# Sums of small products kept in PSUM with ScalarE copies, the products in another order, and the attention's VectorE and ScalarE work at other places

## The chip, the cores and the metric

The kernel runs on one core of one Trainium2 chip. The metric is the device time of one execution in microseconds (us). A core has five engines that run side by side, each through its own list of instructions in order: TensorE (matmul; PE in the profile, PEld its weight loads), VectorE (DVE), ScalarE (ACT), GpSimd (POOL), and SyncE (SP), whose queue issues all DMAs here. Matmul results go to PSUM, eight banks that TensorE, VectorE and ScalarE reach; all else lies in SBUF.

## The reference, cut to what matters

```python
# x: 8 batches x 8 heads x 512 x 64, state: 8 x 8 x 32 x 64
scores = scale * x @ state.T;   a  = softmax(scores);   xread = a @ state
scores2 = scale * state @ x.T;  a2 = softmax(scores2);  sread = a2 @ x
y = concatenate([xread, sread], axis=2)        # per batch 512 + 32 tokens
y = y.transpose(0, 2, 1, 3).reshape(4352, 512) # tokens x 512
h = y @ w_in                                   # 512 x 2048
g = h * sigmoid(1.702 * h)
out = g @ w_out                                # 2048 x 512, float32
```

## The kernel before, in words

**Per batch.** The 512 tokens of a batch (a key: 0 to 7) go through attention, the up product and the down product. Weights of the x side of the attention (a) are not multiplied with state on their own: M = state times w_in is made (att_M, 64 by 32 matmuls, four in the array at a time), and h is a times M. Keys 0 and 1 are computed in a first stage while the weights are unpacked; from key 1's down product on there is one loop over batches, `for b in range(1, B)`. In it the up product of batch b (up_strassen), the down product of batch b (strassen_two) and the attention of batch b + 1 (hooks_next) are interleaved. The last stage ("sr") does the 256 state tokens.

**Up.** up_strassen makes the up product with Strassen's seven products (Winograd's form) instead of eight, four column groups u = 0 to 3, products of 128x256 (L1113), with gelu on ScalarE (L1119, L1159 to L1171) and sums on VectorE (L1122 within it; s12 and s3, L567 to L573, for the sums S1, S2 that the down product needs). In it ScalarE copies one product (L1138) into a bank on which another product then accumulates. `between[u]` holds functions called at the end of group u; they come from `A[b]["sums"]`. Its last product and sums (`rest`) are called inside P1, at hook P1.1.

**Down.** strassen_two makes seven products, P1, P2, P5, P6, P3, P7, P4 in this order, and from key 2 on each of them is itself seven small products (lowly, strassen_low; key 1 has P1 and P2 as whole products, L751). A small product is 4 matmuls of 128x128 in float32, which the profile shows as 8 (L691). In all there are 47 small Strassens. A small Strassen uses three banks x, y, z. The sums of left-hand blocks are VectorE instructions written in line L758 (`tt`): steps1 (P1), steps2 (P2), sums_of(S1), sums_of(S2) and third_of (P5, P6), s4 (the block a12 minus S2), steps12 (P3), steps3 (P7), steps4 (P4). The results of the small products are put together on VectorE (`add`, L696) and ScalarE (L702, L706), with p and u2, two 128x128 pieces of the tile pu, as room for a partial sum.

**Order.** It is written out by hand: every engine works in program order. `at(i)` after the i-th small product calls the functions that belong to the product itself (`own`, `first`) and then the hooks of the name "P2.3", say (P2, after its third small product); "P1", "run" (after P3), "T" (after steps3) are hooks between products. hooks_next(b) fills the names with the attention of the next batch: att_state, att_scores, load_x, att_M 0 and 1, att_blocks (transposes of the scores), then two softmaxes. That of the state side is att_s_max (VectorE), att_s_exp (ScalarE, with a table load, L372), att_s_norm; its result goes out to DRAM and back in another order (eT_out, four issues of 128 KB; eT_in; eT_turn). That of the x side is x_max, x_sub, x_exp (ScalarE, L425), x_sum, x_inverse, x_scale, and x_back, which gives aT. Then the sums of aT and M for the next up stage follow (up_sums: steps 1 to 4 the T-sums of aT; 6 and 9 S1, 7 and 10 S2, 8 and 11 a difference in M's place, 13 and 14 S4).

**Loads.** The next batch's x comes in squares (load_x_squares, L150, 16 issues of 64 KB), issued after P4 into a tile that P4 still read, and VectorE turns them in place (turn_x, L156, four transposes of 128x512). The sums of w_out's blocks for each of the seven products are made once, in key 1's time, and kept in DRAM (`outside`, low_made, low_away); low_load brings three pieces of 256 KB back into one of two rooms (low_a, low_b) each time.

The order of the small products before: q1, q5, q2, q6, q7, q3, q4 in P1 and P2 (`late`), q1, q6, q2, q5, q7, q3, q4 in the others.

Of the kernel before, what the change touches and what calls it, by code (L numbers as in the profile page):

```python
# [10 lines left out]
FP32 = mybir.dt.float32  # L11
# [3 lines left out]
ALU = mybir.AluOpType  # L15
# [5 lines left out]
def kernel(  # L21
# [89 lines left out]

    pu = konst.tile([P, 2, P], FP32, name="pu")
    zeros = free[-1][:, 0].bitcast(mybir.dt.bfloat16)[:, :FC]
# [37 lines left out]

    def turn_x(b):

        A[b]["xT"] = xsq[b]
        for j in range(NPR):
            nc.vector.transpose(xsq[b][:, j], xsq[b][:, j])  # L156
# [487 lines left out]
    def low_load(k, i):  # L644

        for n in (1, 0, 2):
            nc.sync.dma_start(low[:, 3 * i + n], outside[k][:, FC * n : FC * (n + 1)])
# [33 lines left out]

    def strassen_low(left, right, bank, R, at, late=False):

        b11, t3, b21, b22, t1, t2, t4 = right
        a11, a12, a21, a22, s1, s2, s4 = left
        p, u2 = (pu[:, i] for i in range(2))
        x, y, z = (v[:, :P] for v in bank)

        def product(ps, lhs, rhs, first):
            for f in range(QF):  # L690
                nc.tensor.matmul(  # L691
                    ps, lhs[f], rhs[:, f], start=(first and f == 0), stop=(f == QF - 1), skip_group_check=True
                )

        def add(out, x0, x1):
            nc.vector.tensor_tensor(out=out, in0=x0, in1=x1, op=ALU.add)  # L696

        c11, c12, c21, c22 = (R[:, i, P * k : P * (k + 1)] for i in range(2) for k in range(2))

        def q1():  # L700
            product(x, a11, b11, True)
            nc.scalar.copy(p, x)  # L702

        def q2():
            product(x, a12, b21, False)
            nc.scalar.copy(c11, x)  # L706

        def q6():
            product(y, s2, t2, True)
            add(u2, y, p)  # L710

        def q5():
            product(z, s1, t1, True)
            add(c22, z, p)

        def q7():
            product(y, a21, t3, False)
            add(c22, y, c22)

        def q3():  # L720
            product(z, s4, b22, False)
            add(c12, z, u2)

        def q4():
            product(y, a22, t4, False)
            add(c21, y, p)

        for i, q in enumerate((q1, q5, q2, q6, q7, q3, q4) if late else (q1, q6, q2, q5, q7, q3, q4)):
            q()
            at(i + 1)  # L730

    def strassen_two(key, dst, hooks, a4):
# [48 lines left out]

        def sums_of(*pairs):
            for s, (r1, r2, r4) in pairs:
                tt(r1, whole(s, 1, 0), whole(s, 1, 1))
            for s, (r1, r2, r4) in pairs:
                tt(r2, r1, whole(s, 0, 0), ALU.subtract)
            for s, (r1, r2, r4) in pairs:
                tt(r4, whole(s, 0, 1), r2, ALU.subtract)

# [32 lines left out]

        def lowly(name, left, right, kept, banks, R, own, late=False):
            def at(i):
                for fn in own.get(i, ()):
                    fn()
                hook(f"{name}.{i}")

            b11, t3, b21, b22 = halves_of(right)
            strassen_low(left, (b11, t3, b21, b22, *kept), banks, R, at, late)  # L830

# [4 lines left out]
        if key == 1:  # L836
            product(bank(0), A_of(0, 0), B11, "P1")
            nc.scalar.copy(k1, bank(0))
        else:

            m = [mpool.tile([P, NG, FC], FP32, tag=f"M{i}", name="spare_M") for i in range(2)]
            left1, left2 = (v[:, i] for v in m for i in range(2)), None
            w1, w2, w4, p1 = left1
            steps1, left1 = sums(y_of(0, 0), [four(v) for v in (w1, w2, w4)])
            p1 = p1.rearrange("p (r n) -> p r n", r=2)
            for fn in steps1:
                fn()
            o, h0, h1 = low_banks()
            lowly("P1", left1, B11, low_b, [h0, o, h1], p1, {}, True)
            nc.scalar.copy(k1, p1)  # L850
            low_load(5, 1)
            t = apool.tile([P, NG, S], FP32, tag="aT", name="left2_0")
            v = apool.tile([P, NG, SCH, P], FP32, tag="eT", name="left2_1").rearrange("p g c q -> p g (c q)")
            *w, w3 = (four(x[:, i]) for x in (t, v) for i in range(2))
            steps2, left2 = sums(y_of(NU, 0), w, w3)
            for fn in steps2:
                fn()
            hook("P1")
        *r, p5 = spare_M()
        r = [four(v) for v in r]  # L860
        p5 = p5.rearrange("p (r n) -> p r n", r=2)
        if key == 1:
            sums_of((S1, r), (S2, (q1, q2, q4)))
            third_of(S1)
            product(bank(1), A_of(0, 1), B21, "P2")
            tt(osb, bank(1), k1)
        else:
            o, h0, h1 = low_banks()
            own2 = {2: [lambda: sums_of((S1, r))], 4: [lambda: third_of(S1)], 5: [lambda: sums_of((S2, (q1, q2, q4)))]}
            lowly("P2", left2, B21, low_a, [h0, o, h1], osb, own2, True)  # L870
            low_load(2, 0)
            tt(osb, osb, k1)
# [6 lines left out]
        hook("P2")  # L879
        first = [lambda: s4(0), lambda: s4(1), lambda: third_of(S2), lambda: s4(2), lambda: s4(3)]  # L880
        o, h0, h1 = low_banks()

        def at(i):
            for fn in first[i - 1 : i]:
                fn()
            hook(f"P5.{i}")
# [58 lines left out]
    def hooks_next(b):  # L945
# [18 lines left out]
        else:  # L964
            at(p2, att_M1, b)
        at(p2, att_blocks, b)
        at(p2, att_s_max, b)
        at(p2, att_s_exp, b)
        at(p2, eT_out, b)
        at("P2a" if first else "P2", x_max, b, 0)  # L970
        at("P2a" if first else "P2", x_sub, b, 0)
        at("P5.1", x_exp, b, 0)
        at("P5.6", att_s_norm, b)
        at("P5.6", x_max, b, 1)
        at("P5.7", x_sub, b, 1)
        at("P6.1", x_exp, b, 1)
        steps = up_sums(b)

        A[b]["sums"] = {0: steps[9:11], 1: [steps[11], steps[14]]}
        attention = [  # L980
            ("P6.1", x_sum, 0), ("P6.3", x_sum, 1), ("P6.3", x_inverse), ("P6.4", x_scale, 0),
        ]
        attention += [
            ("P6.6", x_scale, 1), ("P3.3", x_back, 0), ("P3.4", x_back, 1), ("P3.5", eT_turn, 0), ("P3.6", eT_turn, 1),
            ("P5", eT_in), ("run", att_sread), ("run", att_M, 3, True), ("run", att_M, 2),
        ]
        names = {"T": range(5), "P7.5": (5, 6), "P7.6": (7,), "P4.1": (8,), "P4.5": (12, 13)}
        for name, fn, *args in attention:
# [351 lines left out]
    for b in range(1, B):  # L1340
# [6 lines left out]
        if b + 1 < B:  # L1347
            if b > 1:
                turn_x(b + 1)
            hooks = hooks_next(b + 1)  # L1350
# [56 lines left out]
```

## Time and profile before

| | |
|---|---|
| time of three runs | 756.40, 758.07, 757.12 us; median 757.12 |
| the profiled execution | 758.99 us, span 757.2 us, mean granted TensorE clock 0.988 |
| busy | PE 705.7, DVE 603.7, ACT 263.6, POOL 0.8 us |
| small products L691 | in groups by tile, 128x128, about 278 ns each, pipelined |
| copies of the small products | L702 264 ns x33 and x14 in another tile, L706 |
| adds of the small products | L696, about 280 ns |
| DMA | 87.39 MB, mean 115 GB/s, 42.0% of 16 engines |

How to read it: the span is the time from the first instruction to the last of one profiled execution. In a timeline row stand start, duration, engine, line, operation, the tile written and those read, the shapes, the count of merged instructions, and in brackets how long the engine stood idle before and what ended it. PE's durations are modelled and overlap: eight matmuls of 128x128 that follow one another start 0.11 us apart. In a row of a window stand its length, busy time and instructions of PE, PEld, DVE, ACT and POOL, then the granted TensorE clock, the share of the DMA engines and GB/s. "issue" as a releaser is time for which the profile shows no other cause.

### The profile page before, as it was taken

To read this page: it belongs to the slowest core of one execution; us is meant where nothing else is said; L and a number is where in the kernel's file an instruction comes from. 1 tells how busy PE (TensorE), PEld (TensorE's weight loads), DVE (VectorE), ACT (ScalarE), POOL (GpSimd) and SP (SyncE) were. 2 spreads that over 40 slices of the span, in tenths; PEclk is the share of its full clock that TensorE was granted. 3 is DMA by queue.
4 is the path that set the end of the run, shared out by engine and by line. 5 is a ranking of instruction groups with operands and counts; after the bars stand their busy time and mean duration, and the time that the engine had idled before them with its cause. 6 is when DMAs were issued, how large, how long until landed. Compare 5 with 4: busy or idle time off the path is not lost.

```text
span 757.2 us, 13522 instructions
## 1 busy us (share of the span) xinstructions
PE 705.7 (93%) x5261; PEld 569.3 (75%) x5263; DVE 603.7 (80%) x1328; ACT 263.6 (35%) x536; POOL 0.8 (0%) x8
## 2 busy tenths in 40 slices
PE   8899999999898899889997999889997999899997
PEld 3333544479786799779985998769986998789995
DVE  6997999999957896869768995789677985688540
ACT  4796410131264224531274125432363126200320
POOL 0000000000000000000000000000000000000000
PEclk9999999999999999999999999999999999899999
DMA  9830344267441764075434744085416540132000
GB/s 231 331 113 28 113 152 103 110 187 176 154 74 54 177 176 106 12 162 156 143 57 98 182 140 101 29 181 168 119 25 133 173 141 16 34 119 82 32 1 29
DMA packets 148527, 87.39 MB, mean 115 GB/s; under 512 B 114416, under 2 KB 128240, under 8 KB 148464
## 3 DMA queue, kind: packets, MB, share of 16 engines
q1 hardware_dynamic: 148464, 86.53, 42.0%
q8 instruction: 42, 0.69, 0.4%
q14 instruction: 21, 0.17, 0.1%
HBM read 68.94 MB, written 17.56 MB: 114 GB/s over the span
## 4 chain that ended last, share of the span: by engine, by line
PE 69%; DVE 17%; ACT 6%; DMA 3%; issue 3%; SPq 0%; DVEq 0%; ACTq 0%
PE low L691 16%; PE o L691 11%; PE o L1113 11%; PE o L544 7%; PE h L526 7%; PE upx L1113 5%; DVE g L758 3%; PE M L320 3%; DVE spare_M L758 3%; PE o L587 2%; PE upw L1113 2%; DVE xsq L156 2%; ACT M L462 1%; ACT e L372 1%; DMA out_dram<-osb 1%
## 5 line engine op out<-in xcount | busy, mean ns | idle before, releaser
L691 PE MATMUL low<-w_out,g 128*128 128x128 f32 x416 | 56.2, 278 | 12.2 <-ACT pu L702 11.2
L691 PEld LDWEIGHTS low<-w_out,g 128*128 128x128 f32 x416 | 51.3, 192 | 17.8 <-ACT pu L702 12.2
L1113 PE MATMUL o<-ta,M 128*128 128x256 f32 x192 | 49.9, 382 | 0.0
L1113 PE MATMUL upx<-aT,M 128*128 128x256 f32 x192 | 49.3, 379 | 0.0
L691 PE MATMUL low<-low,g 128*128 128x128 f32 x336 | 44.4, 275 | 0.0
L702 ACT COPY pu<-low 128x128 f32<-128x128 f32 x33 | 8.7, 264 | 97.7 <-PE low L691 65.2
L691 PEld LDWEIGHTS low<-low,g 128*128 128x128 f32 x336 | 40.9, 192 | 0.0
L1113 PEld LDWEIGHTS o<-ta,M 128*128 128x128 f32 x192 | 35.5, 190 | 6.0 <-ACT g L1159 1.6
L1113 PEld LDWEIGHTS upx<-aT,M 128*128 128x128 f32 x192 | 36.0, 190 | 4.6
L691 PE MATMUL low<-sums,later 128*128 128x128 f32 x280 | 37.9, 279 | 0.9 <-DVE pu L696 0.9
L691 PEld LDWEIGHTS low<-sums,later 128*128 128x128 f32 x280 | 34.6, 194 | 1.9 <-DVE pu L696 1.8
L462 ACT COPY M<-M 128x512 f32<-128x512 f32 x59 | 30.7, 595 | 14.4 <-PE M L320 14.4
L1119 ACT ACTIVATE g<-o 128x512 f32<-128x512 f32 (+1 forms) x56 | 31.3, 559 | 10.7 <-PE o L1113 10.7
L691 PE MATMUL o<-w_out,g 128*128 128x128 f32 x160 | 23.3, 290 | 11.5 <-DVE pu L696 11.5
L691 PEld LDWEIGHTS o<-w_out,g 128*128 128x128 f32 x160 | 20.2, 198 | 17.7 <-DVE pu L696 12.6
L529 ACT ACTIVATE g<-h 128x512 f32<-128x512 f32 x24 | 14.0, 591 | 54.7 <-PE h L526 54.7
L320 PE MATMUL M<-w_in,stT 64*32 64x512 f32 x472 | 31.9, 594 | 0.0
L1122 DVE TENSOR_TENSOR o<-upw,g 128x512 f32<-128x512 f32 x18 | 12.6, 700 | 24.0 <-ACT g L1159 24.0
L526 PE MATMUL h<-low,M 128*128 128x512 f32 x64 | 29.5, 596 | 1.5 <-DVE low L408 1.5
L1113 PE MATMUL o<-ta,ms 128*128 128x256 f32 x120 | 30.8, 379 | 0.0
L526 PE MATMUL h<-aT,M 128*128 128x512 f32 x64 | 28.7, 599 | 1.4 <-ACT M L462 1.4
L691 PE MATMUL low<-low,spare_M 128*128 128x128 f32 x160 | 22.0, 280 | 7.7 <-issue 6.1
(248 smaller groups left out, 1620.1 us busy)
## 6 DMA issues: line engine op xcount, KB each, us to landing
low<-low SPq DMA_DIRECT2D x108, 256.0 KB
low<-low SPq DMA_DIRECT2D x11, 768.0 KB
later<-in_moe_w_out_dram SPq DMA_DIRECT2D x16, 512.0 KB
xn<-in_x_dram SPq DMA_DIRECT2D x28, 256.0 KB
w_out<-in_moe_w_in_dram SPq DMA_DIRECT2D x12, 512.0 KB
xsq<-in_x_dram SPq DMA_DIRECT2D x96, 64.0 KB
out_dram<-osb SPq DMA_DIRECT2D x18, 256.0 KB
out_dram<-later SPq DMA_DIRECT2D x14, 256.0 KB
```

Of the source, the lines that this page charges most:

```text
L156: nc.vector.transpose(xsq[b][:, j], xsq[b][:, j])
L320: nc.tensor.matmul(ps[g][st], A[b]["stT"][rows, st], rhs(rows, j), start=True, stop=True)
L462: nc.scalar.copy(m[:, g], ps[g])
L526: nc.tensor.matmul(hps, lhs[i], rhs[i], start=(i == 0), stop=(i == n - 1))
L529: nc.scalar.activation(out=G[key, f // 2][:, f % 2, :ntok], in_=hps, func=AF.Gelu_apprx_sigmoid)
L544: nc.tensor.matmul(ops, G[key, f // 2][:, f % 2, P * r : P * (r + 1)], w_out[:, f], start=(f == 0), stop=(f == NF - 1))
L587: nc.tensor.matmul(ps[:, r], lhs[f][:, P * r : P * (r + 1)], rhs[:, f], start=(first and r == 0 and f == 0), stop=(f == HF - 1), skip_grou ...
L691: nc.tensor.matmul(ps, lhs[f], rhs[:, f], start=(first and f == 0), stop=(f == QF - 1), skip_group_check=True)
L758: nc.vector.tensor_tensor(out=out, in0=x0, in1=x1, op=op)
L1113: nc.tensor.matmul(ps[:, k], lhs[i][:, o : o + P], rhs[i], start=(first and k == 0 and i == 0), stop=(i == n - 1), skip_group_check=True,)
L1119: nc.scalar.activation(out=dst, in_=src, func=AF.Gelu_apprx_sigmoid)
L1122: nc.vector.tensor_tensor(out=out, in0=ps, in1=x, op=ALU.add)
```

## The change

The three banks now hold the sums as well. ScalarE copies the first product from x into y, and q6 accumulates on it there; z holds q5 and then q3; y holds q1 + q6, then q7 is added, then q4. What was a VectorE add with p or u2 becomes a ScalarE copy of a bank (c22, c12, c21); two adds stay (c22 and c12). The order is q1, q5, q6, q2, q7, q3, q4 in all seven. The tile pu goes, and low_load takes its three pieces in the order 0, 1, 2.

Around it: turn_x of the next batch moves from before P1 into the up stage, two transposes at the end of group 1 and two at the end of group 2. P2's sums (steps2) move from between P1 and P2 into P1. The sums of S1 are spread over P2, and those of S2 move from P2 into P5. The state side's att_s_max goes from P1's end into P2.1, att_s_exp and eT_out to P2.3, att_s_norm from P5.6 to P6.1. The x side moves later as a whole, with x_scale at T and x_back at P7.5, and the up sums move behind it (P7.6 to P4.6).

```diff
-    pu = konst.tile([P, 2, P], FP32, name="pu")
...
-    def turn_x(b):
+    def turn_x(b, *js):
         A[b]["xT"] = xsq[b]
-        for j in range(NPR):
+        for j in js or range(NPR):
             nc.vector.transpose(xsq[b][:, j], xsq[b][:, j])
...
-        for n in (1, 0, 2):
+        for n in range(3):
             nc.sync.dma_start(low[:, 3 * i + n], outside[k][:, FC * n : FC * (n + 1)])
...
-    def strassen_low(left, right, bank, R, at, late=False):
+    def strassen_low(left, right, bank, R, at):
...
-        def q1():
-            product(x, a11, b11, True)
-            nc.scalar.copy(p, x)
-        def q2():
-            product(x, a12, b21, False)
-            nc.scalar.copy(c11, x)
-        def q6():
-            product(y, s2, t2, True)
-            add(u2, y, p)
-        def q5():
-            product(z, s1, t1, True)
-            add(c22, z, p)
-        def q7():
-            product(y, a21, t3, False)
-            add(c22, y, c22)
-        def q3():
-            product(z, s4, b22, False)
-            add(c12, z, u2)
-        def q4():
-            product(y, a22, t4, False)
-            add(c21, y, p)
-        for i, q in enumerate((q1, q5, q2, q6, q7, q3, q4) if late else (q1, q6, q2, q5, q7, q3, q4)):
-            q()
-            at(i + 1)
+        product(x, a11, b11, True)
+        nc.scalar.copy(y, x)
+        at(1)
+        product(z, s1, t1, True)
+        nc.scalar.copy(c22, z)
+        at(2)
+        product(y, s2, t2)
+        nc.scalar.copy(c12, y)
+        at(3)
+        product(x, a12, b21)
+        nc.scalar.copy(c11, x)
+        at(4)
+        product(y, a21, t3)
+        add(c22, y, c22)
+        at(5)
+        product(z, s4, b22)
+        add(c12, z, c12)
+        at(6)
+        product(y, a22, t4)
+        nc.scalar.copy(c21, y)
+        at(7)
...
-        def sums_of(*pairs):
...
+        def sums_of(s, rooms):
+            r1, r2, r4 = rooms
+            return [
+                lambda: tt(r1, whole(s, 1, 0), whole(s, 1, 1)),
+                lambda: tt(r2, r1, whole(s, 0, 0), ALU.subtract),
+                lambda: tt(r4, whole(s, 0, 1), r2, ALU.subtract),
+            ]
...
-            o, h0, h1 = low_banks()
-            lowly("P1", left1, B11, low_b, [h0, o, h1], p1, {}, True)
-            nc.scalar.copy(k1, p1)
-            low_load(5, 1)
...
             steps2, left2 = sums(y_of(NU, 0), w, w3)
-            for fn in steps2:
-                fn()
+            o, h0, h1 = low_banks()
+            own1 = {3: steps2[:1], 4: steps2[1:2], 6: steps2[2:3], 7: steps2[3:]}
+            lowly("P1", left1, B11, low_b, [h0, o, h1], p1, own1)
+            nc.scalar.copy(k1, p1)
+            low_load(5, 1)
             hook("P1")
...
+        sums1, sums2 = sums_of(S1, r), sums_of(S2, (q1, q2, q4))
         if key == 1:
-            sums_of((S1, r), (S2, (q1, q2, q4)))
+            for i in range(3):
+                sums1[i]()
+                sums2[i]()
...
-            own2 = {2: [lambda: sums_of((S1, r))], 4: [lambda: third_of(S1)], 5: [lambda: sums_of((S2, (q1, q2, q4)))]}
-            lowly("P2", left2, B21, low_a, [h0, o, h1], osb, own2, True)
+            own2 = {2: sums1[:1], 4: sums1[1:2], 5: sums1[2:], 6: [lambda: third_of(S1)]}
+            lowly("P2", left2, B21, low_a, [h0, o, h1], osb, own2)
...
-        first = [lambda: s4(0), lambda: s4(1), lambda: third_of(S2), lambda: s4(2), lambda: s4(3)]
+        first = {i + 1: [lambda u=u: s4(u)] for i, u in zip((0, 1, 4, 5), range(NU))}
+        first[3] = [lambda: third_of(S2)]
+        if key > 1:
+            first[1].insert(0, sums2[0])
+            first[2].append(sums2[1])
+            first[4] = sums2[2:]
...
         at(p2, att_blocks, b)
-        at(p2, att_s_max, b)
-        at(p2, att_s_exp, b)
-        at(p2, eT_out, b)
-        at("P2a" if first else "P2", x_max, b, 0)
-        at("P2a" if first else "P2", x_sub, b, 0)
-        at("P5.1", x_exp, b, 0)
-        at("P5.6", att_s_norm, b)
-        at("P5.6", x_max, b, 1)
-        at("P5.7", x_sub, b, 1)
-        at("P6.1", x_exp, b, 1)
+        at("P2a" if first else "P2.1", att_s_max, b)
+        p3 = "P2b" if first else "P2.3"
+        at(p3, att_s_exp, b)
+        at(p3, eT_out, b)
...
+        if b + 1 < B:
+            for i in range(NPR):
+                A[b]["sums"].setdefault(1 + i // 2, []).append((turn_x, (b + 1, i)))
         attention = [
-            ("P6.1", x_sum, 0), ("P6.3", x_sum, 1), ("P6.3", x_inverse), ("P6.4", x_scale, 0),
+            ("P6.1", att_s_norm), ("P6.1", x_max, 0), ("P6.2", x_sub, 0), ("P6.3", x_exp, 0), ("P6.6", x_max, 1),
+            ("P3.1", x_sub, 1), ("P3.3", x_exp, 1), ("P3.4", x_sum, 0), ("P3.5", eT_turn, 0), ("P3.6", eT_turn, 1),
+            ("P3.7", x_sum, 1), ("P3.7", x_inverse),
+            ("P5", eT_in), ("run", att_sread), ("run", att_M, 3, True), ("run", att_M, 2),
+            ("T", x_scale, 0), ("T", x_scale, 1), ("P7.5", x_back, 0), ("P7.5", x_back, 1),
         ]
-        attention += [
-            ("P6.6", x_scale, 1), ("P3.3", x_back, 0), ("P3.4", x_back, 1), ("P3.5", eT_turn, 0), ("P3.6", eT_turn, 1),
-            ("P5", eT_in), ("run", att_sread), ("run", att_M, 3, True), ("run", att_M, 2),
-        ]
-        names = {"T": range(5), "P7.5": (5, 6), "P7.6": (7,), "P4.1": (8,), "P4.5": (12, 13)}
+        names = {"P7.6": range(5), "P4.1": (5, 6), "P4.3": (7,), "P4.5": (8,), "P4.6": (12, 13)}
...
         if b + 1 < B:
-            if b > 1:
-                turn_x(b + 1)
             hooks = hooks_next(b + 1)
```

More of the change, by code (lines that the diff above doesn't have):

```diff
@@ L680, in low_third, with product @@
         T_of(b12, b22, b12)
-    def strassen_low(left, right, bank, R, at, late=False):
+    def strassen_low(left, right, bank, R, at):
         b11, t3, b21, b22, t1, t2, t4 = right
         a11, a12, a21, a22, s1, s2, s4 = left
-        p, u2 = (pu[:, i] for i in range(2))
         x, y, z = (v[:, :P] for v in bank)
-        def product(ps, lhs, rhs, first):
+        def product(ps, lhs, rhs, first=False):
             for f in range(QF):
@@ L821, in sums, with lowly @@
             ], (parts(0, 0), parts(1, 0), parts(0, 1), parts(1, 1), *(blocks(v) for v in rooms))
-        def lowly(name, left, right, kept, banks, R, own, late=False):
+        def lowly(name, left, right, kept, banks, R, own):
             def at(i):
@@ L829, in lowly @@
             b11, t3, b21, b22 = halves_of(right)
-            strassen_low(left, (b11, t3, b21, b22, *kept), banks, R, at, late)
+            strassen_low(left, (b11, t3, b21, b22, *kept), banks, R, at)
         def four(v):
@@ L879, in strassen_two @@
         hook("P2")
[L880 removed]
+        first = {i + 1: [lambda u=u: s4(u)] for i, u in zip((0, 1, 4, 5), range(NU))}
[4 more added lines that the diff above has]
+            first[4] = sums2[2:]
         o, h0, h1 = low_banks()
         def at(i):
[L884 removed]
+            for fn in first.get(i, ()):
                 fn()
```

6 lines of the change are left out of this document (removed).

## The prediction

> **What bounds the kernel now.** I read the page first, then the waits, the chain, and one batch on the timeline of each engine.
>
> ```profile
> span 757.2 us, 13522 instructions
> PE 705.7 (93%) x5261; PEld 569.3 (75%) x5263; DVE 603.7 (80%) x1328; ACT 263.6 (35%) x536; POOL 0.8 (0%) x8
> ```
>
> The page makes TensorE the bound, with at most 7% of the span to win beside any change of its work; this change alters no matmul. The waits (engine, line, releaser; total, times, longest) say who stops it:
>
> ```profile
> PEld o L691 <- DVE pu L696: 18.1, 12, 3.7
> PEld low L691 <- ACT pu L702: 12.2, 5, 2.4
> ```
>
> Both are the small products of L691, waiting for the tile pu. The chain gives the period of a batch, at the same step of five batches' up stage:
>
> ```profile
> 295.03 1.00 PE o L1113 x4
> 378.96 1.00 PE o L1113 x4
> 461.67 1.00 PE o L1113 x4
> 544.39 1.00 PE o L1113 x4
> 628.33 1.00 PE o L1113 x4
> ```
>
> Periods: 83.93 (key 3), 82.71, 82.72 and 83.94 us (key 6). I follow key 4, TensorE's timeline (start, duration; in brackets the wait):
>
> ```profile
> 397.93 1.05 PE L691 MATMUL low<-w_out,g 128*128 128x128 f32 x8
> 398.82 1.03 PE L1113 MATMUL o<-ta,M 128*128 128x256 f32 x4
> 401.38 1.13 PE L691 MATMUL low<-low,spare_M 128*128 128x128 f32 x8 [1.53 <-issue]
> 406.00 1.16 PE L691 MATMUL o<-w_out,g 128*128 128x128 f32 x8 [1.60 <-DVE pu L696]
> 408.88 1.09 PE L320 MATMUL o<-xsq,stT 64*32 64x512 f32 x16
> 411.62 1.16 PE L691 MATMUL low<-w_out,g 128*128 128x128 f32 x8
> 415.94 1.16 PE L691 MATMUL low<-w_out,g 128*128 128x128 f32 x8 [2.25 <-ACT pu L702]
> 421.30 1.06 PE L691 MATMUL low<-sums,later 128*128 128x128 f32 x8
> 428.85 1.06 PE L691 MATMUL low<-sums,later 128*128 128x128 f32 x8
> 444.47 1.16 PE L691 MATMUL o<-w_out,g 128*128 128x128 f32 x8
> 457.19 1.03 PE L1113 MATMUL upx<-aT,M 128*128 128x256 f32 x4
> ```
>
> P1 starts at 397.93, attention at 408.88, P2 at 411.62, P5 at 421.30, P6 at 428.85, P7 at 444.47, the next up stage at 457.19. From 444.47 on, 14 products and one transpose take 12.72 us: 0.9 us each with no stop to speak of. P1 and P2 need 14 x 0.9 = 12.6, the four L1113 matmuls 0.87, attention 2.74, a transpose 0.1: 16.3 us. They take 23.37, so 7.1 us are waiting. P5 takes 7.55 for 6.3 of work: 1.2 more. The rest runs dense. So about 8.3 of the 82.7 us are there to win, all in P1, P2 and P5.
>
> **The change, part by part.** VectorE in key 4:
>
> ```profile
> 390.17 0.70 DVE L1122 TENSOR_TENSOR o<-upw,g 128x512 f32<-128x512 f32 x1 [1.61 <-ACT g L1159]
> 395.35 0.70 DVE L1122 TENSOR_TENSOR o<-upw,g 128x512 f32<-128x512 f32 x1 [1.95 <-ACT g L1159]
> 398.49 2.48 DVE L156 STREAM_TRANSPOSE xsq<-xsq 128x512 f32<-128x512 f32 x4
> 400.89 0.72 DVE L758 TENSOR_TENSOR spare_M<-g,g 128x256 f32<-128x256 f32 x2
> 403.54 0.69 DVE L567 TENSOR_TENSOR later<-g,g 128x512 f32<-128x512 f32 x1
> ```
>
> *Transposes (turn_x).* Four at 0.62 stand ahead of P1's sums; they go two by two into holes of 1.61 and 1.95 us in the up stage: 1.24 fits each, cost nothing, if x has landed. Without that cover VectorE would stand there and hold the L1122 add behind it. The load:
>
> ```profile
> 377.58 8.38 SPq L150 DMA_DIRECT2D xsq<-in_x_dram  x16
> 387.50:388.00 0.50, 0.50 (x5) 0.42 (x4) 0.50 (x2) 0.50 (x2) 0.00 (x0) 1.00 0.00 0
> ```
>
> Issues end at 385.96, and from 387.5 the DMA share (next to last column) is 0.00. The first hole opens at 390.17 - 1.61 = 388.56: 1 us to spare. The load hangs on the end of the previous P4, as the up stage does, so it moves with it.
>
> *P1.* VectorE starts the eight L758 sums at 398.49 instead of 400.89 (2.65 for all), so the first pair is there at 399.2, before TensorE's slot at 398.82 + 0.87 = 399.69. The 1.5 goes. The 1.6 goes too: the product after the first one into y now waits for a ScalarE copy with another product between. Late next is VectorE: 398.49 + 2.65 + 1.95 (three of L567 to L573 at 0.65) + 1.33 (two of the four steps of P2's sums, now inside P1, half of 2.65) = 404.4 before it comes to the add into c22, done at 404.7; the last product's slot, after the ones ahead of it at 0.9, is 404.3. New wait 0.45 (behind it stands all of the attention's TensorE work); the attention starts at about 405.65, 3.2 earlier.
>
> *Seed and copies.* Of five VectorE adds per small Strassen two stay; three become copies, and pu goes: 47 x 3 = 141. The nearest rows:
>
> ```profile
> L702 ACT COPY pu<-low 128x128 f32<-128x128 f32 x33 | 8.7, 264 | 97.7 <-PE low L691 65.2
> L1138 ACT COPY o<-upx 128x512 f32<-128x512 f32 x24 | 13.8, 576 | 26.6 <-PE upx L1113 26.2
> ```
>
> ScalarE gains 141 x 0.264 = 37 us (35 to 40% of the span), beside matmuls. No row copies 128x128 from PSUM to PSUM: between 0.264 and the 0.576 of L1138's four times larger one; I take 0.27, since the form differs from L702 in the target alone and L1138's large copy is no dearer than a common one. Whether the round trip is hidden:
>
> ```profile
> 412.99 1.28 ACT L372 ACT_TABLE_LOAD   x1
> 414.28 0.69 ACT L372 ACTIVATE e<-o,mx 128x512 f32<-128x512 f32 x1
> 415.62 0.26 ACT L702 COPY pu<-low 128x128 f32<-128x128 f32 x1
> 417.13 0.27 ACT L706 COPY osb<-low 128x128 f32<-128x128 f32 x1 [1.25 <-PE low L691]
> ```
>
> The copy at 417.13 starts 0.03 after its product (415.94 + 1.16); the product at 415.94 starts 0.06 after the copy that ends at 415.88. So product, copy, next product is 1.06 + 0.03 + 0.27 + 0.06 = 1.42 us, and with one product between there are 1.79: margin 0.37 (0.06 at 0.576). In ScalarE's queue the waiting seed copy has only the next copies behind it, which need later products anyway, and at P1.1 the last gelu. The add into c22 before the last product has the same distance, as it has now.
>
> *P2.* Today the first copy stands behind four copies of M and the softmax's table load and exps (412.99 to 415.62). The change puts the exps behind the third product. The seed copy then follows the M copies directly, and the 2.25 goes. The exps run between the copies into c12 and c11: P2 starts at 405.65 + 2.74 = 408.4, its third product two slots later ends near 411.35; copy to 411.65; 2.63 of table and exps to 414.3, c11's copy to 414.6. P5's first product reuses that bank, slot about 414.8: just hidden. VectorE has the S1 sums one by one, none late.
>
> *P5.* Its 1.2 was VectorE's, with S2's sums and the attention ahead of the adds. What stands there after the change, five s4 and third steps and three sums at 0.61 and two adds at 0.2, is 5.3 us in 6.3, and no more than two of them between two adds: hidden, and P6 starts at 421.15 instead of 428.85.
>
> *P6 to P4, softmax moved later.* The x part's maxima go to P6, x_scale to T, x_back to P7.5, T-sums to P7.6. The exps of x wait for x_sub, which VectorE does one product earlier, so ScalarE's copies behind them are not held. From P3.6 VectorE has no hole: its second eT_turn ends near 433.9, x_sum and inverse 1.3, four steps3 2.65, two x_scale 1.2, four steps4 2.65, and the add for c22 is done near 442.0; TensorE's slot for P7's last product is 442.2. Two x_back 1.3, the add 0.2, four T-sums 1.5, then in P4 five sums of 0.6, and its add at 448.1 against a slot at 448.5. Hidden, by 0.2 and 0.4; without that cover each 0.1 is paid in full. M's third and S4 come after it, and the up stage needs them only at its fifth and seventh product, 4 us on.
>
> *DMA queue.* eT_out stays ahead of low_load(2, 0), which P6's second product now needs at about 422. eT_out issues when the exps end, 414.5 for some 3 us; 512 KB at the rate of the x load (1 MB from 377.6 to 387.5) is 5 us, so the first low tile lands near 421. Margin 1 us; today it is 7. The new order of its three pieces is the order of use.
>
> *The sum.* Key 4: 23.37 + 7.55 become 16.3 + 0.45 + 6.4 and 0.1 of restart: 7.7 us. Keys 2 to 6: 38.5. Keys 3 and 6 lose their extra 1.2 as well:
>
> ```profile
> 333.00:336.80 3.80, 3.42 (x18) 3.12 (x17) 2.18 (x4) 0.27 (x1) 0.00 (x0) 0.55 0.93 137
> 647.29 1.05 PE L691 MATMUL low<-w_out,g 128*128 128x128 f32 x8
> 655.41 2.07 PE L691 MATMUL o<-w_out,g 128*128 128x128 f32 x8 [3.52 <-DVE pu L696]
> 655.50:660.50 5.00, 5.00 (x24) 5.00 (x25) 0.58 (x2) 0.00 (x0) 0.00 (x0) 0.50 0.00 0
> 670.40 1.47 PE L691 MATMUL low<-sums,later 128*128 128x128 f32 x8
> ```
>
> In key 3's row the granted clock is 0.55 right after the waits of P1 and P2. With these gone, 2 x 1.2 = 2.4.
>
> Key 7 has no attention; P1 and P2 take 23.1 us (647.29 to 670.40) for 13.5 of work. The clock is 0.50 for 5 us behind a wait of 3.5, which costs 2.5. VectorE has four more sums at P1.2 there (2.4), so by key 4's count, 249.36 later, the add is done at 404.7 + 2.4 + 249.4 = 656.5, against a slot at 653.6: 2.9 of wait stay. P2's wait goes, and of the slow clock I keep half, 1.25, since the wait before it is a little shorter: 23.1 - 13.5 - 2.9 - 1.25 - 0.1 = 5.3.
>
> Key 1 has no small P1 and P2, and VectorE is its bound in P7 and P4:
>
> ```profile
> 189.15 0.68 DVE L1275 TENSOR_TENSOR low<-w_out 128x512 f32<-128x512 f32 x1
> 191.81 0.75 DVE L758 TENSOR_TENSOR later<-g,g 128x256 f32<-128x256 f32 x2
> ```
>
> low_made and low_third take 2.66 us (189.15 to 191.81) ahead of P7's sums and as much again inside P4. x_scale and x_back (2.5), and the later x_sum and inverse (1.3), join them; six adds (1.2) leave, and M's third and S4 (1.2) move behind P4. So VectorE comes to P4's last adds about 1.4 us later than today, and TensorE with it: -1.5.
>
> Sum: 38.5 + 2.4 + 5.3 - 1.5 = 44.7. The profiled execution had 758.99 (span 757.2), 0.25% above the median 757.12 of three. 758.99 - 44.7 = 714.3; against the median 712.4. I say 713.
>
> **Rivals.** *VectorE takes TensorE's place as bound.* For it: the margins 0.2 and 0.4 in P7 and P4 and the 0.45 in P1. If it comes 1 us late there and at P3, 2 to 3 us per batch return, 10 to 18 in all: 723 to 731.
>
> *A queue delays P5 or P6.* The exps hold c11's copy, or eT_out holds the low tiles beyond the 1 us: 1 to 2 us per batch for five, 718 to 723.
>
> *The round trip decides, slower than before.* If accumulating on a bank that ScalarE wrote costs much more than the 1.42, every small Strassen pays twice (seed, copy of y): 47 x 2 x the excess over 1.79. It eats the 44 us when the copy takes 0.37 + 0.47 longer, 1.1 us; at 1.3 the time is 757 - 44 + 62 = 775. L1138's 0.576 and the dense up stage that uses such a seed speak against it.
>
> *No change.* All of the 7.7 per batch would have to come back as waits of other engines; VectorE's case at 2.5 times its price would do it, and no row shows that much.
>
> *The clock stays whole in key 7.* If a wait of 2.9 us is too short to halve it, the 1.25 kept above goes: 711.5. For it: 2.9 is shorter than the 3.5 of today. Against it: key 3's 0.55 came after several shorter waits close together. The Trainium skill, "TensorE: Matmul & The Clock Gate", Part 1, has the clock halve after an idle window of about 3.4 us and come back after a busy one as long; by that rule this rival would hold, while key 3's row does not fit so sharp an edge.
>
> **How the numbers follow.** The forecast (709 to 717) has 0.45, the whole clock 0.15, VectorE as bound 0.2, a queue 0.11, slower 0.06, no change 0.03. A difference within 0.2% (1.5 us) can't be told from none here. With no new wait in keys 2 to 6 (0.55 x 5), none in key 1 and the whole clock the time would be about 706; the range goes from there to the end of VectorE's case, 705 to 731. Faster 0.91, same 0.03, slower 0.06.
>
> **What would show it.** The waits on pu are gone; L691 waits total under 10 us in keys 2 to 6. Periods near 75.0, equal for keys 3 to 5, granted clock 1.00 there. P1 keeps about 0.5 before its last product, released by VectorE. L156 stands in the up stage with no wait on DMA. ScalarE near 300 us busy, VectorE near 575. Wrong if L691 waits for ScalarE, for low tiles at P6, or if VectorE's add releases the last product late in P7 and P4.

## The result, and the profile after

The changed kernel takes 718.0 us (median; 717.4 to 718.5). Against 757.4 us of the kernel before on the same chip the ratio is 0.9481, interval 0.9464 to 0.9497: 5.2% faster. The forecast was 713, range 705 to 731. The profiled execution had 717.44 us, span 715.7, so 41.5 us of span went where the sum had 44.7.

The page after, busy times of the engines:

```profile
span 715.7 us, 13574 instructions
PE 692.5 (97%) x5263; PEld 562.2 (79%) x5263; DVE 570.0 (80%) x1187; ACT 298.8 (42%) x677; POOL 0.8 (0%) x8
```

ScalarE's 141 more instructions (536 to 677) and 35.2 us more are the copies, VectorE's 141 fewer the adds; the forecast had 37 and "near 300" and "near 575". TensorE's busy share rose from 93 to 97%, with the same matmuls. Its waits at the small products, now L689 (engine, line, releaser; total, times, longest), and the step of the chain that gave the period before:

```profile
PE o L689 <- DVE spare_M L694: 4.7, 6, 2.9
PE low L689 <- DMA low<-low: 2.4, 2, 2.2
PE low L689 <- DVE g L694: 2.4, 1, 2.4
PE low L689 <- DVE later L694: 1.6, 1, 1.6
```

```profile
214.14 0.99 PE o L1104 x4
252.98 4.53 DMA low<-low
289.54 1.00 PE o L1104 x4
364.89 1.00 PE o L1104 x4
439.87 1.00 PE o L1104 x4
514.85 1.00 PE o L1104 x4
553.72 6.53 DMA low<-low
592.27 1.00 PE o L1104 x4
```

The waits on pu (18.1 and 12.2) are gone. Of the first row 2.9 are key 7's and the other five 0.36 each, in keys 2 to 6; with the DMA's 2.4 these keys wait 4.2 us, where the forecast had under 10. The last two rows are key 1's. The periods are 75.40 (key 2), 75.35, 74.98, 74.98 and 77.42 us (key 6), where before they were 82.7 to 83.9. One thing is new: in keys 2 and 6 a DMA for the low tiles stands in the chain, where none stood in these keys before.

Key 4 on TensorE's timeline, from P1 (383.86) to the next up stage (435.39):

```profile
383.86 1.05 PE L689 MATMUL low<-w_out,g 128*128 128x128 f32 x8
385.61 1.05 PE L689 MATMUL low<-low,spare_M 128*128 128x128 f32 x8
388.40 1.06 PE L689 MATMUL o<-w_out,g 128*128 128x128 f32 x8
390.70 1.16 PE L689 MATMUL o<-low,g 128*128 128x128 f32 x8 [0.36 <-DVE spare_M L694]
394.53 1.16 PE L689 MATMUL low<-w_out,g 128*128 128x128 f32 x8
400.91 1.06 PE L689 MATMUL low<-sums,later 128*128 128x128 f32 x8
407.16 1.06 PE L689 MATMUL low<-sums,later 128*128 128x128 f32 x8
422.67 1.16 PE L689 MATMUL o<-w_out,g 128*128 128x128 f32 x8
435.39 1.03 PE L1104 MATMUL upx<-aT,M 128*128 128x256 f32 x4
```

The brackets of 1.53, 1.60 and 2.25 are gone, and one of 0.36 stands ahead of P1's last product. P1 to P5 takes 400.91 - 383.86 = 17.05 us, from 23.37; P5 takes 6.25, from 7.55; P6 to P7 15.51, from 15.62, and P7 to the up stage 12.72, as before.

Where the 41.5 us came from, with the same marker of the chain in every kernel (the step printed above, first at 214.14):

| us | before | sums alone | places alone | changed |
|---|---|---|---|---|
| start to key 1's marker | 212.3 | 211.8 | 217.0 | 214.1 |
| keys 2 to 6 | 416.0 | 400.1 | 392.6 | 378.1 |
| key 7 and the last stage | 128.9 | 120.4 | 126.9 | 123.4 |

The columns "sums alone" and "places alone" are the first two experiments.

### The profile page after: what moved, and what is told of

It reads as the page before. It is cut to its first block, busy times and chain, and to the rows that moved or that the text cites. A ratio compares the mean times of both kernels' runs of the same rounds, so it can differ in the third digit from the quotient of the medians.

```text
span 715.7 us, 13574 instructions
## 1 busy us (share of the span) xinstructions
PE 692.5 (97%) x5263; PEld 562.2 (79%) x5263; DVE 570.0 (80%) x1187; ACT 298.8 (42%) x677; POOL 0.8 (0%) x8
## 4 chain that ended last, share of the span: by engine, by line
PE 82%; DVE 11%; DMA 3%; ACT 2%; issue 1%; SPq 0%; DVEq 0%; ACTq 0%
PE low L689 22%; PE o L689 12%; PE o L1104 12%; PE o L543 8%; PE h L525 7%; PE upx L1104 5%; PE M L319 4%; PE o L586 2%; PE upw L1104 2%; PE o L738 2%; DMA low<-low 2%; DVE spare_M L745 1%; PE o L319 1%; DVE later L567 1%; PE warm L124 1%; DVE g L745 1%
## 5 line engine op out<-in xcount | busy, mean ns | idle before, releaser
L689 PE MATMUL low<-w_out,g 128*128 128x128 f32 x416 | 55.2, 279 | 0.0
L689 PEld LDWEIGHTS low<-w_out,g 128*128 128x128 f32 x416 | 51.4, 195 | 4.5 <-issue 4.2
L689 PE MATMUL low<-low,g 128*128 128x128 f32 x336 | 43.7, 276 | 6.3 <-DMA low<-low 2.4
L689 PEld LDWEIGHTS low<-low,g 128*128 128x128 f32 x336 | 40.3, 192 | 7.2 <-issue 2.9
L689 PE MATMUL low<-sums,later 128*128 128x128 f32 x280 | 35.8, 275 | 0.0
L689 PEld LDWEIGHTS low<-sums,later 128*128 128x128 f32 x280 | 33.6, 192 | 0.1
L543 PE MATMUL o<-w_out,g 128*128 128x512 f32 x64 | 28.5, 594 | 0.0
L543 PE MATMUL o<-w_out,sums 128*128 128x512 f32 x64 | 28.3, 592 | 0.0
L1150 ACT COPY g<-o 128x512 f32<-128x512 f32 (+1 forms) x28 | 15.6, 555 | 25.6 <-PE o L1104 25.4
L525 PEld LDWEIGHTS h<-aT,M 128*128 128x128 f32 x64 | 11.8, 190 | 18.3 <-issue 12.2
L689 PE MATMUL o<-low,g 128*128 128x128 f32 x152 | 21.3, 285 | 4.7 <-DVE spare_M L694 4.7
```

The source lines that it names most:

```text
L525: nc.tensor.matmul(hps, lhs[i], rhs[i], start=(i == 0), stop=(i == n - 1))
L543: nc.tensor.matmul(ops, G[key, f // 2][:, f % 2, P * r : P * (r + 1)], w_out[:, f], start=(f == 0), stop=(f == NF - 1))
L689: nc.tensor.matmul(ps, lhs[f], rhs[:, f], start=(first and f == 0), stop=(f == QF - 1), skip_group_check=True)
L1150: nc.scalar.copy(c12, Y(u))
```

## The experiments

**The new small Strassen alone** (psum_only: the sums in PSUM, the copies and the new order of products in the kernel before, attention and sums where they were).

```diff
 # kernel before, with the new body of strassen_low (three lines written as one)
-        for i, q in enumerate((q1, q5, q2, q6, q7, q3, q4) if late else ...):
+        product(x, a11, b11, True); nc.scalar.copy(y, x); at(1)
+        product(z, s1, t1, True); nc.scalar.copy(c22, z); at(2)
...
```

> The kernel before with the new small Strassen alone (sums in PSUM, new order, pieces loaded in the order of use); all attention and VectorE work stays where it was. My theory: the 1.5 us wait in P1 is the transposes ahead of its sums and P2's 2.3 us is the softmax's exps ahead of ScalarE's first copy, so both stay; only P1's second wait (1.6), most of P5's 1.2 and 0.5 in P2 go. Period of keys 2 to 6 about 79.5 instead of 82.7, time 735 to 741. Rival, the sums in PSUM carry the gain and the new places only tidy up: period 76 or less, time 720 to 726.

Measured: 734.23 us, ratio 0.9684 (0.965 to 0.9718), span 732.3: 0.8 us below the theory's range, far from the rival's. What TensorE still waits for in key 3:

```profile
313.61 1.13 PE L689 MATMUL low<-low,spare_M 128*128 128x128 f32 x8 [1.53 <-issue]
326.31 1.16 PE L689 MATMUL o<-low,left 128*128 128x128 f32 x8 [2.26 <-ACT o L698]
```

The 1.60 of P1 is gone: that product no longer needs VectorE's add into pu. The 1.53 ahead of P1's second product stays, and so does P2's wait, as 2.26. It is P2's third product in both kernels: before, it waited for the ScalarE copy into pu that empties its bank, now it waits for the copy into o on which it accumulates, and both copies stand behind the same softmax instructions. A PSUM sum doesn't help while the copy that makes it is queued behind the exps.

**The new places alone** (places_only: the changed kernel with the old small Strassen and pu).

```diff
-        product(x, a11, b11, True); nc.scalar.copy(y, x); at(1)
...
+        for i, q in enumerate((q1, q5, q2, q6, q7, q3, q4) if late else ...):
```

> The changed kernel with the old small Strassen (pu, five VectorE adds, two copies, the old orders of products and of low pieces), the work around it at its new places. My theory: the waits behind transposes and exps are gone without the PSUM sums as well; P1 keeps about 1.5 us for VectorE's adds behind the sums, and the three adds more per small Strassen (0.6 us) use up the margins of 0.2 and 0.4 us in P7 and P4. Period about 77.5, time 725 to 733. Rival, the places bring nothing without the ScalarE copies: 745 or more.

Measured: 738.15 us, 0.9728 (0.9687 to 0.9768), span 736.4: slower than the range. Its TensorE rows in keys 3 and 7:

```profile
320.82 1.16 PE L691 MATMUL o<-w_out,g 128*128 128x128 f32 x8 [1.67 <-DVE pu L696]
637.29 2.08 PE L691 MATMUL o<-w_out,g 128*128 128x128 f32 x8 [4.19 <-DVE pu L696]
```

In keys 2 to 6 it gave 23.4 us; of P1's and P2's waits those for VectorE's adds are left, 1.67 in P1 and 0.38 in P2. What was missed lies at the ends: VectorE keeps five adds per small Strassen, and key 1's marker comes 4.7 us later, of which 1.7 are a stretch of half clock (granted clock 0.50 from 209.42 to 212.83); key 7 has a 4.19 us wait. The two halves of the change are 15.9 and 23.4 us in keys 2 to 6, 39.3 together, and the whole gave 37.9: in the steady keys they add up almost fully, as each removes other waits. In key 1 the sums take load off VectorE and the places put it on: -0.5 and +4.7 alone (+3.0 without the half clock), +1.8 together. In key 7 and the last stage the sums alone give 8.5 us, more than the whole change's 5.5: the wait ahead of P1's last product is 1.53 there, and 2.88 with the new places too.

**One part undone each.** turn_back puts the four transposes back ahead of P1; exps_back puts the maxima, exps and eT_out of the state side back to P1's end.

```diff
 # turn_back
-                A[b]["sums"].setdefault(1 + i // 2, []).append((turn_x, (b + 1, i)))
...
+            if b > 1:
+                turn_x(b + 1)
 # exps_back
-        at("P2a" if first else "P2.1", att_s_max, b)
-        p3 = "P2b" if first else "P2.3"
+        at(p2, att_s_max, b)
+        p3 = "P2b" if first else p2
```

> The changed kernel with the four transposes of the next batch's x back ahead of P1's sums. My theory: VectorE comes 2.4 us later to its add in P1 in keys 2 to 6, and the wait before P1's last small product grows from 0.36 to about 2.8 us: 718 + 5 x 2.4 = 730 us, a little more if the granted clock falls. Rival, the transposes hide behind other waits of P1: 718 to 720.

> The changed kernel with the state side's maxima, exps and their way out to DRAM back at the end of P1, ahead of P2. My theory: the seed copy of P2 stands behind table load and exps on ScalarE again, P2's third small product waits some 2.3 us in keys 2 to 6; the DMA wait at P6 of key 6 (2.2 us in the profile) goes, since the state side goes out earlier. 718 + 11.5 - 2 = 727 us. Rival, with a product between the seed and its use ScalarE has room for the exps: 716 to 718.

Measured: turn_back 732.04 us, 0.9649 (0.9608 to 0.969), span 729.0; exps_back 733.22 us, 0.9666 (0.9631 to 0.9701), span 730.0. turn_back in key 4:

```profile
393.86 1.13 PE L689 MATMUL low<-low,spare_M 128*128 128x128 f32 x8 [1.53 <-issue]
399.62 1.16 PE L689 MATMUL o<-low,g 128*128 128x128 f32 x8 [0.96 <-DVE spare_M L694]
```

The 1.53 that the profile had put down to "issue" is back to the hundredth: it is VectorE's first sum, behind the transposes (in key 2 the profile names it: 1.58, released by VectorE's spare_M). The add before the last product comes later too, 0.96 for 0.36. Together 2.1 of the 2.4 by which the period grew (77.35 in keys 4 and 5). So the price was as expected, but not the place: the expectation had all of it ahead of P1's last product, as 2.8.

exps_back has the 2.26 of psum_only in every key, but not the same price: the period is 77.51 in key 4 and 79.13 in key 3. Two such waits on TensorE's timeline, then the windows right behind them (length, busy times, and the granted clock third from the end):

```profile
327.41 1.98 PE L689 MATMUL o<-low,left 128*128 128x128 f32 x8 [2.26 <-ACT o L698]
406.55 1.16 PE L689 MATMUL o<-low,left 128*128 128x128 f32 x8 [2.26 <-ACT o L698]
```

```profile
327.40:330.40 3.00, 2.99 (x14) 2.99 (x15) 0.00 (x0) 0.42 (x2) 0.00 (x0) 0.53 0.69 103
406.50:409.50 3.00, 2.95 (x26) 2.95 (x27) 0.00 (x0) 0.72 (x3) 0.00 (x0) 1.00 0.72 114
```

After the same wait the clock was 0.53 in key 3 and 1.00 in key 4; in keys 2, 5 and 6 it was below 0.65, as in key 3. Half clock over 3 us costs 1.5, which is the difference of the periods (1.6). Four keys of five at 1.6 are 6.4, and the miss of exps_back (expected near 727) is this. The wait for the low tiles in key 6 is gone, as expected.

**The seed of a sum, made longer.** seed_x4 does ScalarE's seed copy four times; only its length changes.

```diff
-        nc.scalar.copy(y, x)
+        for _ in range(4):
+            nc.scalar.copy(y, x)
```

> The changed kernel with ScalarE's seed copy done four times over in every small Strassen, which leaves the result as it is. It measures the margin of the round trip (product, copy, product 1.42 of 1.79 us by the rows). A copy repeated adds between 0.16 and 0.27 us, so 0.5 to 0.8 for three more; over the margin of 0.37 by 0.1 to 0.45, in 47 small Strassens: 5 to 20 us slower than the changed kernel, with waits of TensorE for the seed. Rival, ScalarE's copies are far from deciding: no difference. Other rival, the round trip is already at its limit: 25 to 38 us slower.

Measured: 736.11 us, 0.972 (0.9703 to 0.9737), 16.25 us above the changed kernel on the same chip. P6 of key 4 on TensorE, then the four copies on ScalarE:

```profile
415.97 1.06 PE L689 MATMUL low<-sums,later 128*128 128x128 f32 x8
416.87 1.06 PE L689 MATMUL low<-low,g 128*128 128x128 f32 x8
418.22 1.16 PE L689 MATMUL o<-low,g 128*128 128x128 f32 x8 [0.30 <-ACT o L699]
```

```profile
417.07 1.10 ACT L699 COPY o<-low 128x128 f32<-128x128 f32 x4 [0.63 <-PE low L689]
```

Product 1.06, 0.04, four copies 1.10, 0.05: the accumulating product starts 2.25 after the first. One copy is a quarter of 1.10, 0.28 (the row that the prediction lacked, PSUM to PSUM), so the round trip is 1.43 against the slot of 1.79: the margin of 0.37 was right (0.36). The period grew by 3.46 (78.44), 0.49 per small Strassen for 2.25 - 1.79 = 0.46 of excess: what goes over the slot is paid in full here, and in the changed kernel, where the copy stays under it, TensorE waits for no seed in keys 2 to 6.

**The low tiles.** In the changed kernel key 6 waits for a DMA at P6's second product; the other 0.2 of the DMA's 2.4 is key 2's:

```profile
560.39 1.13 PE L689 MATMUL low<-low,g 128*128 128x128 f32 x8 [2.20 <-DMA low<-low]
```

SP's queue in keys 4 and 6, then the windows right behind eT_out (the last three columns are clock, DMA share, GB/s):

```profile
400.59 3.09 SPq L469 DMA_DIRECT2D squares<-e  x4
403.78 2.08 SPq L646 DMA_DIRECT2D low<-low  x3
550.56 3.06 SPq L469 DMA_DIRECT2D squares<-e  x4
553.72 2.12 SPq L646 DMA_DIRECT2D low<-low  x3
```

```profile
403.60:406.60 3.00, 3.00 (x29) 3.00 (x28) 3.00 (x7) 0.54 (x2) 0.00 (x0) 1.00 0.98 176
553.60:556.60 3.00, 3.00 (x30) 3.00 (x29) 2.99 (x7) 0.53 (x2) 0.00 (x0) 1.00 0.98 151
```

In both keys the low tiles are issued 3.2 us after eT_out's first issue, and the engines are 0.98 busy; but 176 GB/s go through in key 4 and 151 in key 6. The forecast's margin of 1 us held in keys 3 to 5, fell short by 0.2 in key 2 and broke in key 6: by the chain the tiles took 6.53 us from 553.72 on, and TensorE's slot came after 4.3. split_load issues two of the three pieces at the same step, P2.3, ahead of the exps and of eT_out:

```diff
-            own2 = {2: sums1[:1], 4: sums1[1:2], 5: sums1[2:], ...}
-            low_load(2, 0)
+            own2 = {2: sums1[:1], 4: sums1[1:2], 3: [lambda: low_load(2, 0, (0, 1))], 5: sums1[2:], ...}
+            low_load(2, 0, (2,))
```

old_pieces leaves the place and takes the pieces in the old order 1, 0, 2.

> The changed kernel with the first two of the three low pieces for P6 issued in P2.3, ahead of eT_out in the DMA queue, and the third after P2 as now. My theory: the wait at P6 (2.2 us in key 6, 0.2 in key 2 of the profile) is the pieces' place behind eT_out's small packets, so it goes: 1 to 3 us below the changed kernel. Rival, the wait is slow DMA in that stretch whatever the order: no difference, with a DMA wait in P6 of some key.

> The changed kernel with low_load's three pieces in the old order 1, 0, 2, so that the piece of P6's second small product comes second. My theory: that piece lands about 1.1 to 1.4 us later (408.5 in place of 407.1 in key 4 of the changed kernel's trace) against a slot at 408.06, so P6's second product waits 0.4 us or more in keys 2 to 6, by DMA: 2 to 4 us slower than the changed kernel, 720 to 723. Rival, both pieces are there in time and the order is free: no difference.

Measured: split_load 716.61 us, 0.9463 (0.9445 to 0.948), beside 719.86, 0.9506 (0.9489 to 0.9523), of the changed kernel once more on that chip (after_again); old_pieces 722.03, 0.9517 (0.9494 to 0.9539).

> The changed kernel itself, beside the next ones on one chip: 717 to 719 us.

split_load's queue in key 6, then its chain:

```profile
546.61 1.50 SPq L646 DMA_DIRECT2D low<-low  x2
549.92 3.24 SPq L469 DMA_DIRECT2D squares<-e  x4
553.25 0.70 SPq L646 DMA_DIRECT2D low<-low  x1
```

```profile
214.25 0.99 PE o L1104 x4
514.22 1.00 PE o L1104 x4
589.20 1.00 PE o L1104 x4
```

Its keys 2 to 6 take 374.95 us, 75.0 each, and key 6 (514.22 to 589.20) is like the rest. The changed kernel has 378.1 there in its first profile and 380.2 in after_again, where key 3's tiles stand in the chain as well as key 6's. So it is the late issue of these pieces, and 3.2 to 5.3 us come back; the 5.3 holds 1.7 of half clock behind after_again's wait of 2.03 in key 6 (granted clock 0.50 from 562.05 to 565.46). split_load changes two things together, the place ahead of eT_out and with it the time of issue, 7 us earlier. A place behind eT_out need not cost a wait: in exps_back the pieces are issued 3.15 us after eT_out's first issue as well (566.14 after 562.99 in key 6), but P6's second product starts 10.3 us later, at 576.46, and doesn't wait. The Trainium skill, "DMA: Bandwidth & Descriptors", section "Queues, rings and completion order", says that each DMA engine takes the descriptors of a ring in their order; the two queues above fit that, 2.20 of wait behind eT_out and none ahead of it, without proving it. The total fell by 3.2 only, since its key 7 and last stage take 125.1, against 123.4 in both profiles of the changed kernel; most of this is the clock, as shown below. In old_pieces all of keys 2 to 6 wait at that product, 0.7 to 2.2 us; the order 0, 1, 2 in the change is not cosmetic. Keys 2 to 6 take 382.0 there, against 378.1 and 380.2; the total was taken on another chip, and its ratio is not told apart from after_again's.

**Two versions with the remaining waits taken out.** p1_sums, on top of split_load, moves the second of P2's sums from P1.4 to P1.5, and in key 7 the four more sums from P1.2 to P2.1 and P2.3. best also moves key 1's low_made and low_third out of the stretch around P7 and P4 into and before the next up stage, where VectorE has holes.

```diff
 # p1_sums
-            own1 = {3: steps2[:1], 4: steps2[1:2], 6: steps2[2:3], 7: steps2[3:]}
+            own1 = {3: steps2[:1], 5: steps2[1:2], 6: steps2[2:3], 7: steps2[3:]}
-            ahead["P1.2"] = [steps[i] for i in (0, 1, 4, 5)]
+            ahead["P2.1"] = [steps[i] for i in (0, 1)]
+            ahead["P2.3"] = [steps[i] for i in (4, 5)]
 # best
-        if key == 1:
-            low_made(0, B11, 1)
-            low_third(B11)
...
+            if b == 2:
+                low_made(0, B11, 1)
+                low_third(B11)
+            more = [(low_made, (1, B21, 0)), (low_third, (B21,))] if b == 2 else []
```

> The version best without its edit to key 1: the split load, P1's second step of P2's sums after the add, and key 7's four other sums in P2. It tells the parts of best apart: by its traces key 1's edit is worth 4.5 us, so 706 to 707; P1 and key 7 together are then 9 to 10 us against the split load alone (716.6). Rival, key 1's edit is the larger part: 709 or more.

> A version meant to beat both: the split load; in P1 the second step of P2's sums after the add into c22; key 7's four other sums from P1.2 to P2.1 and P2.3; key 1's low_made and low_third, twice, out of P7 and P4 into VectorE's holes of the next up stage. By the changed kernel's trace: 0.36 x 5 in P1, 2.9 of wait and 1.7 of slow clock in key 7, 0.4 + 1.6 + 2.4 in key 1, 2.4 at P6: 13 us, time 703 to 708. Rival, the waits move on to the next product (VectorE has no room in P2 of key 7 and in the up stage of key 2): 710 to 716.

Measured: p1_sums 707.03 us, 0.9332 (0.931 to 0.9353); best 702.01 us, 0.9266 (0.9251 to 0.9281), the fastest here and 1 us under its range. best's span is 700.8 us, TensorE busy in 98% of it. Its chain:

```profile
209.72 1.00 PE o L1098 x4
581.66 1.00 PE o L1098 x4
```

Keys 2 to 6 take 371.94, 74.4 each, key 1's marker stands 4.4 us earlier than after the change, key 7 and the last stage take 119.1. p1_sums has 214.19 at the marker and the same 371.85 and 119.2, so its two edits are worth 9.1 us of span (714.3 to 705.2, two chips) and key 1's edit 4.4. Of the 9.1, 3.1 are in keys 2 to 6 and 5.9 in key 7 and the last stage, where neither the wait nor a half clock is left.

## Why the prediction was right, and where 3 us were missing

**Keys 2 to 6** (38.5, and 2.4 of clock: 40.9). The period in keys 4 and 5 came out at 74.98 where 75.0 was forecast, 7.7 less than before, and each part showed by itself: the 1.53 returns with the transposes alone, the 2.25 with the exps alone, the 1.60 went with the PSUM sums. The clock's 2.4 came too: in split_load keys 3 and 6 fell by 8.9 and 9.0 us, key 4 by 7.7. The 0.45 of new wait in P1 is the bracket of 0.36. The step that was mis-sized is *DMA queue*: "Margin 1 us" was left out of the sum, put to one rival. It was too little by 0.2 in key 2 and by 2.2 in key 6. split_load, without it, gained 41.1 us in these keys, the 40.9 of the sum; the 0.3 to 0.4 that keys 2 and 3 had over 75.0 went too.

**P2 and P5.** VectorE's and ScalarE's order after the change in key 4 (ScalarE's rows, then VectorE's):

```profile
400.46 0.26 ACT L707 COPY osb<-low 128x128 f32<-128x128 f32 x1
402.06 0.25 ACT L698 COPY low<-low 128x128 f32<-128x128 f32 x1 [0.68 <-PE low L689]
```

```profile
374.40 1.30 DVE L155 STREAM_TRANSPOSE xsq<-xsq 128x512 f32<-128x512 f32 x2
384.42 0.75 DVE L745 TENSOR_TENSOR spare_M<-g,g 128x256 f32<-128x256 f32 x2
```

c11's copy ends at 400.72, and P5's first product starts at 400.91: "just hidden" was right, by 0.2. The PSUM to PSUM seed of P5 takes 0.25 and starts 0.09 after its product (400.91 + 1.06). The transposes stand in the up stage, the first two at 374.40 with no bracket, and P1's first two sums are done at 385.17, ahead of the second product at 385.61.

**The rivals.** VectorE as the bound in P7 and P4 (0.2 and 0.4 of margin) didn't come in keys 2 to 6: P7 to the next up stage is 12.72, the same as before. The queue rival came, though with weight in one key of five and not in all. The round trip and "no change" did not.

**Key 7** (5.3). The table's last row fell by 5.5; P1 and P2 alone take 18.1 us (611.24 to 629.38), 5.0 less than 23.1. The wait forecast as 2.9 was 2.88 (timeline, then the window behind it):

```profile
620.50 1.72 PE L689 MATMUL o<-low,g 128*128 128x128 f32 x8 [2.88 <-DVE spare_M L694]
```

```profile
620.50:625.50 5.00, 5.00 (x30) 5.00 (x31) 2.78 (x7) 1.40 (x4) 0.00 (x0) 0.66 0.20 56
```

Over 5 us at 0.66 some 1.7 are lost, for the 1.25 kept in the sum; so in this profile the rival "the clock stays whole" falls, though the wait is shorter than the window of about 3.4 us in the Trainium skill, "TensorE: Matmul & The Clock Gate", Part 1. The page has that window free-running. The traces agree with the window's length (3.41 us), but here 2.03 us of idle within one window were enough. How much is lost differs. In exps_back the same wait in key 7, 2.87, left the clock at 1.00, so that the rival fell is partly luck. Behind split_load's wait of 2.87 in key 7 the clock was 0.50 for longer, and 3.0 were lost (four products took 6.54 us from 617.42 on, at 0.89 each 3.57):

```profile
617.40:621.80 4.40, 4.38 (x20) 4.38 (x21) 2.79 (x7) 1.14 (x3) 0.00 (x0) 0.50 0.18 63
```

**Key 1** (-1.5). It cost 1.8, and it is VectorE, as said: the waits of 1.6 and 2.4 shown above, at adds of P7 and P4, where four waits of 2.0 us together stood before. best, which takes 5.3 us of VectorE's work out of that stretch, wins 4.4 there.

So 37.9 + 5.5 - 1.8 stand for 40.9 + 5.3 - 1.5: the 3 us are the low tiles' late issue. The forecast of 713 and the measured 718.0 are 5 us apart. Nearly all of the other 2 is that the waits were read from an execution of 758.99, 1.9 above the median from which the forecast subtracts them.

## What to carry to other kernels

Find each wait's own cover before you move work, and price the steady period and the first and last key apart: here two edits added up in the steady keys, while at the ends the same engine's load made one edit lose what another won. A product that accumulates on a seed copied by another engine is free as long as product, copy and both handovers fit the slot that one product in between leaves (1.43 of 1.79 us); here 0.46 over it cost 0.49. A transfer with a margin of 1 us behind another batch in its queue belongs ahead of that batch, where it is issued earlier. A wait of 2 us or more on TensorE can cost up to 3 us of slow clock on top.

## What of the hardware was not expected

Waits of the same length are not the same price: 2.26 us left TensorE's clock whole in key 4 of exps_back and took it to 0.53 in key 3, and 2.88 gave 0.66 over 5 us. The traces show what decides it. In each of the twelve profiles, from 60 us on to 25 us before the end, the granted clock falls to 0.50 only for 3.41 us or twice that, and these stretches start whole multiples of 3.413 us apart. The run can so be laid out in windows of 3.41 us (idle is the window's length less TensorE's busy time in it):

| run, key | wait, us | idle of TensorE in the windows that the wait touches | clock in the next window |
|---|---|---|---|
| exps_back, key 3 | 2.26 | 2.26 (324.15 to 327.56) | 0.50 |
| exps_back, key 4 | 2.26 | 1.77, then 0.49 (402.65 to 406.06 to 409.48) | 1.00 |
| changed kernel, key 6 | 2.20 | 1.30, then 0.90 (556.07 to 559.49 to 562.90) | 1.00 |
| after_again, key 6 | 2.03 | 2.03 (558.64 to 562.05) | 0.50 |
| changed kernel, key 7 | 2.88 | 2.88 (617.51 to 620.92) | 0.50 |
| exps_back, key 7 | 2.87 | 1.14, then 1.73 (631.34 to 634.76 to 638.17) | 1.00 |

Of the windows at full clock, all 19 with 2.03 us idle or more were followed by half clock, and none with 1.77 or less; in between both came (1.79 and 1.82 half, 1.90 whole). So a wait of 2 to 3 us costs nothing more when a window's edge divides it in the middle, and about 1.7 us when it falls into one window. Behind split_load's wait the clock stayed at 0.50 for a second window; 0.78 us of the wait lay in the first. Where the edges lie differs from one execution to the next: the half clock in key 7 began 0.42 us after the wait's end in the changed kernel's profile and 0.89 after it in after_again. Key 3's 0.55 before the change, which the prediction put down to several shorter waits, is the same: 2.07 of the 2.25 us of P2's wait lie in the window that ends at 333.34, where the half clock begins.

The DMA engines, 0.98 busy in both, moved 176 GB/s in key 4 and 151 in key 6 with the same issues; why key 6 is slower stays open. It was slower in the two profiles of the changed kernel and in old_pieces (waits of 2.0 to 2.2 us at that product).
